# Eagle attention and MLP on one Trainium2 core: a new written order, two small loads moved to ScalarE's queue, and fewer DMA transposes

## The chip, the cores and the metric

The kernel runs on one core of a Trainium2 chip. The core has a matrix engine (TensorE, PE in the profile), three engines for elementwise work (VectorE or DVE, ScalarE or ACT, GpSimd or POOL), a sequencer that here only starts transfers (SyncE, SP), and DMA engines that move data between the chip's memory and the on-chip buffer. Each engine works through its own list of instructions in order; semaphores hold an instruction until what it needs is there. The metric is the device time of one execution in microseconds (us). Smaller is better.

## The reference

There are two stages. The first is a linear attention with a decaying state, for 4 batches, 8 heads, 768 steps and a head size of 48:

```python
for t in range(S):
    cur = einsum('bhd,bhe->bhde', u * k[t], v[t])
    y[t] = einsum('bhd,bhde->bhe', r[t], state + cur)
    state = w[..., None] * state + einsum('bhd,bhe->bhde', k[t], v[t])
```

The second takes y as rows of 384 numbers (8 heads of 48) and gives `x + relu(norm(x) @ w_ch1) @ w_ch2`, where norm subtracts the row's mean, divides by its standard deviation and multiplies by `g_ln`. The inner width is 1536. The output is 4 x 768 x 384 in float32.

## The kernel before

**Tiles.** The 768 steps of a batch are cut into 6 chunks of 128, so there are 24 chunks in all, and each chunk is a tile of 128 rows. Within a chunk the recurrence becomes matrix products: the decay is moved into the factors `Fk` and `Fr`, so that k and r only have to be multiplied by a table. A state `Z` is handed from each chunk to the next one of the same batch.

**Steps of a chunk i**, each a short function with the name used in the written order:

- LK, LR, LV load k, r and v (192 KB each, lines 315, 318, 321) on SP's queue.
- SK and SR multiply k and r by their tables (`sck`, `scr`); CV casts v to bfloat16 (`vv`). All three can be given to VectorE or GpSimd, CV to ScalarE too.
- TR turns `scr` and `sck` on TensorE (8 transposes, line 337); TC copies the result out of PSUM, or TCr and TCk half of it each (`trs`). For the chunks in `K_BY_DMA` (18 to 23) the keys are turned by a DMA instead (TKD, line 476).
- Q multiplies the turned r and k (`q`); AT forms the 128 x 128 products per head (line 356); AM masks them (line 366), for the first chunks in two halves AMa and AMb.
- S forms the diagonal term with u and the chunk's state contribution in PSUM; CC copies out the diagonal term; VB multiplies v by it on GpSimd (line 419).
- ZU takes the state contribution out of PSUM. For most chunks ZU adds the old state on VectorE (line 413) and ZD multiplies by the decay on GpSimd. For the first chunk of a batch, and for a chunk in `ZPE`, ZU is one multiplication on VectorE; for a chunk in `ZPE` the old state has been added by one more matmul in S (line 394), and there is no ZD.
- Y applies the state and the masked products (lines 429 and 437); X adds VB's result (`x`).
- ST and AG give mean and variance (lines 447 and 451), XN subtracts the mean (`xn`), and RS raises the variance to the power -1/2 on GpSimd, once for each group.
- LT turns `xn` on TensorE (3 transposes, line 481) and XT copies the result into `xT`; or LTD does both with one DMA transpose on SP's queue (line 472).

**MLP by groups.** Chunks form groups of one or two, in the list `GROUPS`. For a group, UP multiplies by the first weights (line 496): six steps of 6 matmuls with 256 columns for a group of two, three steps of 12 matmuls with 128 columns for a group of one. RL is the relu that copies 128 x 512 out of PSUM (line 512). DN multiplies by the second weights (line 524), in three parts of 4 matmuls for each chunk. OT scales by RS's result and adds x (line 534); STO stores the chunk on SP's queue. UP's number is 16 times the group plus the part, DN's is 4 times the chunk plus the part.

**Start.** WF loads w as a row, LN takes its logarithm, WBM spreads it over the partitions, FK and FR make the tables. ROWS loads w and u with head pairs down the partitions (`w_p`, `u_p`), four small transfers on SP's queue (line 214); UW and WL make from them the matrix for u and the decay table `WLZ`. LW1 loads a third of the first weights (768 KB), and SW multiplies a third of that third by -g and casts it. IW2 loads a third of the second weights from GpSimd's queue (line 312). WU and DU are matmuls of zeros that keep TensorE busy (line 260).

**The order.** There is no loop over chunks. The string `PLAN` lists every step with its number and its engine (v, s or g for VectorE, ScalarE, GpSimd; a dash where the engine is fixed), and the program emits the steps as they stand there. An engine's instructions follow in that order; each waits only for its data and its buffer. Buffers are rings whose sizes are in `SLOTS`; the change leaves them as they are.

Of the kernel before, what the change touches and what calls it, by code (L numbers as in the profile page):

```python
# [25 lines left out]
LT,0,- AT,2,- VB,1,g XT,0,s SW,2,v SW,0,s DU,3,- UP,2,- Q,2,v X,1,v UP,0,- RL,2,s
ST,1,v UP,1,- AG,1,v RL,0,s ZU,1,v RS,1,g XN,1,v DN,0,- RL,1,s AM,2,v LT,1,- DN,1,-
ZD,1,g XT,1,v S,2,- UP,16,- CC,2,v LK,3,- ZU,2,v UP,17,- VB,2,g RL,16,s LR,3,- DN,2,-
ZD,2,g SK,3,v UP,18,- OT,0,v LR,5,- Y,2,- SR,3,v DN,4,- RL,17,s LV,3,- RL,18,s X,2,v
TR,3,- DN,5,- ST,2,v LR,4,- TC,3,v DN,6,- CV,3,g AG,2,v Q,3,v LK,4,- AT,3,- XN,2,v  # L30
S,3,- SR,4,g SR,5,v LT,2,- LK,5,- XT,2,s CC,3,v RS,2,g ZU,3,v UP,32,- SK,4,v LV,5,-
UP,34,- OT,1,v RL,32,s AM,3,v TR,4,- VB,3,g LV,4,- DN,8,- CV,5,s TC,4,s SK,5,v LR,7,-
Y,3,- UP,33,- ZD,3,g X,3,v CV,4,s TR,5,- LR,6,- Q,4,v ST,3,v AT,4,- SR,7,g RL,33,s
S,4,- AM,4,v RL,34,s LK,6,- DN,9,- TC,5,s SR,6,g DN,10,- AG,3,v LK,7,- XN,3,v Y,4,-
Q,5,v LT,3,- CC,4,v AT,5,- SK,6,v RS,3,g LR,9,- XT,3,s ZU,4,v TR,6,- VB,4,g AM,5,v
S,5,- LR,16,- UP,48,- CC,5,s TC,6,s ZD,4,g UP,50,- SK,7,v LV,6,- RL,48,s X,4,v TR,7,-
VB,5,g RL,50,s OT,2,v Y,5,- LR,8,- TC,7,s UP,49,- ST,4,v X,5,v DN,12,- LK,8,- RL,49,s
AG,4,v ST,5,v AT,6,- XN,4,s Q,6,v DN,13,- LK,15,- AG,5,v AM,6,v XN,5,s RS,4,g LT,4,-
DN,14,- XT,4,s LR,10,- SK,8,g CV,6,v LT,5,- AT,7,- Q,7,v XT,5,s S,6,- SR,8,v LK,9,-
Y,6,- UP,67,- CC,6,v AM,7,v VB,6,g UP,64,- LV,7,- RL,67,s ZU,6,v TR,8,- RL,64,s X,6,v  # L40
UP,66,- LV,9,- TC,8,s SR,9,v UP,65,- CV,7,v STO,0,- RL,66,s Q,8,v AT,8,- CV,9,g LV,8,-
ST,6,v Y,7,- RL,65,s UP,68,- SK,9,v OT,3,v LK,10,- S,7,- RL,68,s TR,9,- AG,6,v SR,10,v
CC,7,s UP,69,- CV,8,s VB,7,g LR,11,- AM,8,v XN,6,s DN,16,- RL,69,s DN,17,- STO,1,- TC,9,s
ZU,7,v STO,2,- X,7,v DN,18,- ZD,7,g SK,10,v LR,13,- LT,6,- S,8,- ST,7,v XT,6,s AT,9,-
Y,8,- CC,8,v OT,4,v LR,14,- TR,10,- SR,11,g ZU,8,v DN,20,- TC,10,s AG,7,v LV,10,- Q,9,v
VB,8,g DN,21,- XN,7,v AM,9,v LT,7,- LV,17,- RS,5,g S,9,- DN,22,- XT,7,v ZD,8,g AT,10,-
LK,11,- Q,10,v UP,81,- X,8,v OT,5,v UP,80,- CC,9,s LV,11,- RL,81,s VB,9,g AM,10,v Y,9,-
RL,80,s UP,84,- LR,12,- SK,11,g ZU,9,v UP,82,- RL,84,s SR,13,v CV,11,g LK,12,- TR,11,- X,9,v
RL,82,s ZD,9,g DN,24,- ST,8,v TC,11,s LV,19,- UP,83,- CV,10,v SR,12,g AG,8,v XN,8,v Y,10,-
LV,16,- Q,11,v RL,83,s LT,8,- SK,12,g S,10,- ST,9,v UP,85,- CC,10,v AG,9,v LK,13,- ZU,10,v  # L50
XN,9,s VB,10,g DN,25,- XT,8,v RL,85,s AT,11,- LK,17,- X,10,v LT,9,- RS,6,g DN,26,- XT,9,v
AM,11,v UP,100,- LR,21,- ZD,10,g S,11,- UP,99,- SK,13,v LK,14,- RL,100,s TR,12,- CC,11,v ST,10,v
UP,101,- TC,12,v STO,3,- RL,99,s Y,11,- AG,10,v SK,14,g STO,5,- Q,12,v TR,13,- SR,14,v LR,22,-
UP,96,- TC,13,s OT,6,v SR,16,g AT,12,- XN,10,v STO,4,- DN,28,- RL,96,s AM,12,v VB,11,g LV,12,-
RL,101,s LT,10,- DN,29,- XT,10,s X,11,v UP,97,- LV,13,- ST,11,v TR,14,- RL,97,s CV,12,v UP,98,-
LV,21,- AG,11,v TC,14,v XN,11,s AT,13,- Q,13,v S,12,- LR,15,- RL,98,s AM,13,v LT,11,- Y,12,-
XT,11,s DN,30,- CC,12,s LV,15,- RS,7,g ZU,12,v UP,116,- SK,15,v UP,114,- VB,12,g LV,14,- OT,7,v
AT,14,- SR,15,v RL,114,s CV,13,g DN,32,- LK,16,- AM,14,v RL,116,s TR,15,- UP,117,- TC,15,s LV,22,-
Q,14,v UP,112,- CV,14,v X,12,v RL,117,s LR,17,- S,13,- CV,15,v Y,13,- RL,112,s ST,12,v DN,33,-
Q,15,v CV,17,g CC,13,s STO,6,- ZU,13,v UP,113,- LV,18,- VB,13,g SK,16,v S,14,- RL,113,s CV,16,v  # L60
DN,34,- AG,12,v CC,14,v LK,18,- X,13,v XN,12,s ZD,13,g TR,16,- SK,17,v AT,15,- TC,16,s LK,19,-
ST,13,v UP,115,- VB,14,g OT,8,v Y,14,- RL,115,s ZU,14,v LT,12,- LK,22,- DN,36,- XT,12,v AG,13,v
Q,16,v S,15,- RS,8,g LK,20,- DN,37,- XN,13,v SK,18,v LT,13,- DN,38,- CC,15,v XT,13,v STO,7,-
VB,15,g AM,15,v UP,128,- STO,8,- ZD,14,g LV,20,- UP,129,- RL,128,s OT,9,v AT,16,- X,14,v RL,129,s
DN,40,- LR,19,- SR,17,v Y,15,- ST,14,v DN,41,- LR,20,- AM,16,v DN,42,- STO,9,- UP,130,- X,15,v
LR,18,- OT,10,v UP,132,- SR,19,v TR,17,- LK,23,- RL,132,s AG,14,v ZU,15,v DN,44,- SR,18,g XN,14,v
RL,130,s S,16,- LK,21,- ST,15,v DN,45,- ZD,15,g CV,19,v AG,15,v UP,133,- TC,17,v LR,23,- RS,9,g
CC,16,v DN,46,- SK,19,v RL,133,s Q,17,v LTD,14,- VB,16,g UP,131,- XN,15,s CV,18,v LV,23,- OT,11,v
Y,16,- TR,18,- ZU,16,v RL,131,s DN,48,- X,16,v STO,10,- DN,49,- TCr,18,v LTD,15,- ZD,16,g SR,21,v
S,17,- TKD,18,- TR,19,- ST,16,v DN,50,- STO,11,- CV,20,v UP,149,- SR,22,v TKD,19,- TCr,19,v UP,145,-  # L70
RL,149,s OT,12,v AT,17,- AG,16,v RL,145,s CC,17,v SR,20,v DN,52,- XN,16,s AM,17,v UP,147,- VB,17,g
STO,12,- DN,53,- Q,18,v RL,147,s Y,17,- SK,20,v UP,146,- Q,19,v CV,21,v AT,18,- X,17,v DN,54,-
RL,146,s ST,17,v UP,144,- LTD,16,- OT,13,v S,18,- RL,144,s UP,148,- AG,17,v CC,18,v RS,10,g XN,17,v
# [12 lines left out]
X,22,v DN,77,- ST,22,v RL,194,s DN,78,- AG,22,v XN,22,v RS,13,g UP,197,- OT,19,v STO,18,- UP,195,-
RL,197,s DN,80,- LTD,22,- RL,195,s Y,23,- STO,19,- DN,81,- X,23,v DN,82,- ST,23,v UP,208,- AG,23,v
OT,20,v RS,14,g UP,209,- XN,23,v DN,84,- DN,85,- RL,209,s LTD,23,- RL,208,s DN,86,- UP,210,- STO,20,-
OT,21,v UP,224,- RL,210,s DN,88,- DN,89,- STO,21,- RL,224,s DN,90,- UP,225,- OT,22,v UP,226,- RL,225,s
DN,92,- RL,226,s DN,93,- STO,22,- DN,94,- OT,23,v STO,23,-  # L90
"""


@with_exitstack
def kernel(
    ctx: ExitStack,
    tc: tile.TileContext,
    r: bass.AP,
# [20 lines left out]
    FK = F // P  # L119
# [59 lines left out]
    w_p = const.tile([P, HP], FP32, name="w_p")  # L179
    u_p = const.tile([P, HP], FP32, name="u_p")  # L180
# [401 lines left out]
```

## Time and profile before

| what | value |
|---|---|
| median of 3 runs | 164.08 us (163.05 to 164.20) |
| the profiled execution, its own time | 164.15 us |
| its span in the profile | 162.4 us |
| TensorE busy | 148.9 us (92%), 1823 matmuls |
| VectorE busy | 131.5 us (81%), 282 instructions |
| ScalarE busy | 72.4 us (45%), 129 instructions |
| GpSimd busy | 73.1 us (45%), 102 instructions |
| moved by DMA | 24.48 MB, mean 151 GB/s |

The span is the time from the first to the last recorded instruction; the execution's own time is 1.75 us more. A busy TensorE is not TensorE at its peak, because each matmul is recorded with its whole passage through the array, and these overlap. In lines of groups, the numbers after the bar are the busy time of the group, the mean of one instruction in ns, and the idle time of the engine before them with what ended it. In lines of the timeline, the first two numbers are start and duration in us, and a bracket tells how long the engine stood idle before and what released it. "x12" is the number of instructions merged in one line.

### The profile page before, as it was taken

What the parts mean: (1) busy time and instruction counts of PE and PEld (TensorE: products, weight loads), DVE (VectorE), ACT (ScalarE), POOL (GpSimd) and SP (SyncE); (2) the same over time, 40 slices, a digit from 0 to 9 for tenths busy, and PEclk for the clock granted to TensorE, in tenths of its full rate; (3) what the DMA queues carried; (4) which work ended last, traced back from release to release, by engine and by line L of the source; (5) the groups of instructions that cost most, each with busy time, mean ns of one, the idle gap of its engine ahead of it and who ended that gap; (6) DMA issues with size and microseconds to landing.
All of it is one profiled execution on the core that took longest, in us unless ns stands there. A gap on an engine that the chain in (4) does not pass through costs nothing.

```text
span 162.4 us, 4487 instructions
## 1 busy us (share of the span) xinstructions
PE 148.9 (92%) x1823; PEld 120.2 (74%) x1823; DVE 131.5 (81%) x282; ACT 72.4 (45%) x129; POOL 73.1 (45%) x102
## 2 busy tenths in 40 slices
PE   7998699989999999999999899899899799999690
PEld 6797578767869868868888678678588587877570
DVE  2378777899999999999998999999998995715111
ACT  4203753438586853646566123353146152442220
POOL 3001725775844299886328637521254727211000
PEclk9999969999999999999999999999999999999998
DMA  4999997989999994994889998552322423120311
GB/s 90 220 223 257 320 215 149 213 158 179 177 199 229 240 189 97 220 261 82 178 167 219 221 202 165 125 160 57 86 71 70 77 47 117 52 73 22 105 48 48
DMA packets 88646, 24.48 MB, mean 151 GB/s; under 512 B 84017, under 2 KB 87090, under 8 KB 88626
## 3 DMA queue, kind: packets, MB, share of 16 engines
q1 hardware_dynamic: 88194, 23.02, 62.7%
q0 software_dynamic: 432, 1.18, 3.7%
q8 instruction: 14, 0.23, 0.6%
q14 instruction: 6, 0.05, 0.1%
HBM read 18.88 MB, written 4.72 MB: 145 GB/s over the span
## 4 chain that ended last, share of the span: by engine, by line
PE 40%; DVE 34%; DMA 11%; SPq 6%; issue 4%; ACT 2%; POOL 1%; DVEq 0%; POOLq 0%
PE hp L496 18%; PE o L524 15%; DMA xT<-xn 6%; DVE A L366 6%; DMA w_f<-in_moe_w_ch_dram 4%; DVE q L202 4%; DVE ot L534 4%; DVE sck L202 3%; DVE x L444 3%; DVE stats L447 3%; DVE ZS L413 3%; DVE xn L459 2%; DVE scr L202 2%; PE at L356 2%; SPq L315 1%
## 5 line engine op out<-in xcount | busy, mean ns | idle before, releaser
L512 ACT ACTIVATE hT<-hp 128x512 bf16<-128x512 f32 x72 | 42.1, 597 | 57.0 <-PE hp L496 56.1
L496 PE MATMUL hp<-xT,w_sb 128*128 128x256 bf16 (+1 forms) x540 | 57.0, 255 | 3.2 <-DMA xT<-xn 2.7
L524 PE MATMUL o<-w_sb,hT 128*128 128x384 bf16 x288 | 56.0, 326 | 1.4 <-DVE ot L534 1.4
L496 PEld LDWEIGHTS <-w_sb 128*128 128x128 bf16 x540 | 48.3, 115 | 6.8 <-DMA xT<-xn 3.2
L524 PEld LDWEIGHTS <-hT 128*128 128x128 bf16 x288 | 25.9, 97 | 14.3 <-issue 1.7
L419 POOL TENSOR_TENSOR Vb<-vf,cc 128x384 f32<-128x384 f32 x24 | 22.7, 947 | 19.2 <-DVE cc L199 14.0
L366 DVE TENSOR_TENSOR A<-at,mask 128x1024 bf16<-128x1024 f32 (+1 forms) x26 | 29.4, 1129 | 1.3 <-PE at L356 1.3
L534 DVE SCALAR_TENSOR_TENSOR ot<-o,rs,x 128x384 f32<-128x384 f32 x24 | 14.6, 609 | 12.5 <-PE o L524 12.3
L202 POOL TENSOR_TENSOR Z<-ZS,WLZ 128x384 bf16<-128x384 f32 x16 | 17.0, 1064 | 6.5 <-DVE ZS L413 6.5
L202 DVE TENSOR_TENSOR sck<-kf,Fk 128x384 bf16<-128x384 f32 x19 | 13.1, 693 | 4.0 <-ACT Fk L274 4.0
L444 DVE TENSOR_TENSOR x<-y,Vb 128x384 f32<-128x384 f32 x24 | 13.1, 547 | 3.5 <-PE y L437 2.1
L260 PE MATMUL o<-warm 128*128 128x128 bf16 x143 | 13.2, 267 | 1.0 <-DVE warm L225 1.0
L465 POOL TENSOR_SCALAR rs<-mv 128x2 f32<-128x2 f32 (+1 forms) x15 | 3.9, 259 | 22.3 <-DVE mv L451 22.1
L197 ACT COPY trs<-tr 128x1024 bf16<-128x1024 bf16 (+1 forms) x12 | 11.8, 980 | 4.5 <-PE tr L337 4.4
L260 PEld LDWEIGHTS <-warm 128*128 128x128 bf16 x143 | 11.6, 123 | 2.5 <-issue 1.3
L447 DVE BATCH_NORM_STATS2 stats<-x 128x6 f32<-128x384 f32 x24 | 13.3, 553 | 0.2
L202 DVE TENSOR_TENSOR q<-trs 128x512 bf16<-128x512 bf16 x24 | 12.5, 523 | 0.0
L468 POOL TENSOR_TENSOR rs<-rs,expo 128x2 f32<-128x2 f32 (+1 forms) x15 | 10.5, 697 | 1.2
L202 POOL TENSOR_TENSOR scr<-rf,Fr 128x384 bf16<-128x384 f32 x7 | 8.1, 1169 | 5.7 <-DMA rf<-in_r_dram 4.8
L202 DVE TENSOR_TENSOR scr<-rf,Fr 128x384 bf16<-128x384 f32 x17 | 9.7, 573 | 0.8 <-DMA rf<-in_r_dram 0.8
L356 PE MATMUL at<-trs 48*128 48x128 bf16 x192 | 9.7, 222 | 0.4 <-DMA trs<-sck 0.4
L337 PE MATMUL tr<-ident,scr 128*128 128x128 bf16 x96 | 9.5, 223 | 0.3 <-ACT xT L197 0.2
(60 smaller groups left out, 162.0 us busy)
## 6 DMA issues: line engine op xcount, KB each, us to landing
rf<-in_r_dram SPq DMA_DIRECT2D x24, 192.0 KB, 3.8
kf<-in_k_dram SPq DMA_DIRECT2D x24, 192.0 KB, 3.9
vf<-in_v_dram SPq DMA_DIRECT2D x24, 192.0 KB, 3.8
out_dram<-ot SPq DMA_DIRECT2D x24, 192.0 KB, 2.4
w_f<-in_moe_w_ch_dram SPq DMA_DIRECT2D x3, 768.0 KB, 7.2
w_sb<-in_moe_w_ch_dram POOLq DMA_DIRECT2D x3, 384.0 KB, 7.7
xT<-xn SPq DMA_TRANSPOSE x10, 2.4
trs<-sck SPq DMA_TRANSPOSE x6, 2.4
```

The costliest lines, as they stand in the source:

```text
L197: nc.scalar.copy(out=out, in_=in_)
L202: engines[e].tensor_tensor(out=out, in0=in0, in1=in1, op=ALU.mult)
L260: nc.tensor.matmul(out=warm_ps[0][:, :P], lhsT=warm[:], rhs=warm[:], start=True, stop=True)
L356: nc.tensor.matmul(out=t[:, par, q, :], lhsT=trs(i)[p0 : p0 + D, 1, q, :], rhs=trs(i)[p0 : p0 + D, 0, q, :], start=True, stop=True,)
L366: nc.vector.tensor_tensor(out=AA(i)[:, a:b].rearrange("p e q t -> p (e q) t"), in0=psum["at", i][:, a:b].rearrange("p e q t -> p (e q) t") ...
L419: nc.gpsimd.tensor_tensor(out=Vb(i)[:].rearrange("p (h d) -> p h d", h=H), in0=vf(i)[:], in1=cc(i)[:].unsqueeze(2).to_broadcast([P, H, D]) ...
L444: nc.vector.tensor_tensor(out=xx(i)[:], in0=psum["y", i][:, :C], in1=Vb(i)[:], op=ALU.add)
L447: nc.vector.bn_stats(out=stats[i % 4][:], in_=xx(i)[:])
L496: nc.tensor.matmul(out=t[:, a * gw : (a + 1) * gw], lhsT=w1_sb[n][kc][:, fb::FB], rhs=xT(g)[:, kc, :gw], start=(kc == 0), stop=(kc == CK - 1),
L512: nc.scalar.activation(out=o, in_=s, func=ACT.Relu)
L524: nc.tensor.matmul(out=psum["o", i][:, :C], lhsT=hT(g)[:, fk, j * P : (j + 1) * P], rhs=w2_sb[d][:, a, :], start=(fk == 0), stop=(fk == FK ...
L534: nc.vector.scalar_tensor_tensor(out=ot(i)[:], in0=psum["o", i][:, :C], scalar=rs[g][:, j : j + 1], in1=xx(i)[:], op0=ALU.mult, op1=ALU.add,)
```

## The change

Nothing changes in what is computed. These things do:

- `GROUPS` has 12 groups of one and 6 of two, where it had 6 and 9. The groups of one are the chunks 0 to 7 and 20 to 23.
- `ZPE` is [1, 2, 3], where it was empty.
- ROWS becomes ROWSI: the same four small transfers, u first, issued by ScalarE. It stands after LN and before FK in the order.
- LTD is not used any more: the 10 chunks 14 to 23 that it served use LT and XT like the others. TKD stays for the chunks 18 to 23.
- There are 105 matmuls of zeros instead of 143.
- The whole order is another one, and many steps have another engine:

| step | before | after |
|---|---|---|
| SK | 19 VectorE, 5 GpSimd | 12, 12 |
| SR | 17 VectorE, 7 GpSimd | 8, 16 |
| CV | 15 VectorE, 4 ScalarE, 5 GpSimd | 5, 13, 6 |
| Q | 24 VectorE | 18, 6 GpSimd |
| XN | 14 VectorE, 10 ScalarE | 3, 15, 6 GpSimd |
| XT | 6 VectorE, 8 ScalarE | 14, 10 |
| TC (whole) | 5 VectorE, 11 ScalarE | 10, 6 |
| TCr and TCk (halves) | 9 VectorE, 1 ScalarE | 3, 7 |
| CC | 15 VectorE, 9 ScalarE | 8, 16 |
| RL | 72 ScalarE | 68, 4 VectorE |
| SW | 3 VectorE, 6 ScalarE | 2, 6, 1 GpSimd |
| ZD | 16 GpSimd | 13 |
| RS | 15 GpSimd | 18 |

```diff
-GROUPS = [1, 1, 1, 1, 2, 2, 2, 2, 2, 2, 2, 2, 2, 1, 1]
-ZPE = []
+GROUPS = [1, 1, 1, 1, 1, 1, 1, 1, 2, 2, 2, 2, 2, 2, 1, 1, 1, 1]
+ZPE = [1, 2, 3]
 K_BY_DMA = [18, 19, 20, 21, 22, 23]
...
-MW,0,v WF,0,- MI,0,g TL,0,s WU,19,- LR,1,- MP,0,v MM,0,g LK,1,- LN,0,s DU,4,- WBM,0,-
-LK,0,- LR,2,- FK,0,s LR,0,- SK,0,v FR,0,s LV,0,- SK,1,v SR,0,v LK,2,- SR,1,v DU,35,-
-TR,0,- CV,0,v TCk,0,v LG,0,- TCr,0,v LV,2,- SK,2,v DU,13,- TR,1,- SR,2,v AT,0,- LW1,2,-
-TCk,1,v AMa,0,v TCr,1,v Q,0,v DU,18,- TR,2,- AMb,0,v ROWS,0,- CV,2,v LW1,1,- DU,4,- Y,0,-
-Q,1,v AT,1,- UGC,0,s UW,0,g SW,7,s SW,8,v WL,0,s AMa,1,v IW2,0,g DU,7,- S,0,- CC,0,s
-LV,1,- SW,6,s ZU,0,v VB,0,g SW,5,s LW1,0,- IW2,1,g X,0,v SW,4,s ST,0,v CV,1,s AMb,1,v
-IW2,2,g SW,3,s DU,38,- S,1,- AG,0,v TC,2,v Y,1,- XN,0,s RS,0,g SW,1,v CC,1,s DU,2,-
-LT,0,- AT,2,- VB,1,g XT,0,s SW,2,v SW,0,s DU,3,- UP,2,- Q,2,v X,1,v UP,0,- RL,2,s
...
+MW,0,v WF,0,- TL,0,s MI,0,g MP,0,v WU,13,- MM,0,g LN,0,s LK,0,- ROWSI,0,s WBM,0,- LV,1,-
+LR,0,- FK,0,s CV,1,v FR,0,s SK,0,v LK,1,- SR,0,g LR,1,- SK,1,v DU,18,- TR,0,- UW,0,g
+WL,0,s LK,2,- SR,1,g TCk,0,s LR,2,- TCr,0,s SK,2,g Q,0,v DU,22,- TR,1,- LV,0,- AT,0,-
+TCk,1,s SR,2,v LG,0,- LW1,2,- TCr,1,s AMa,0,v CV,0,g UGC,0,s AMb,0,v DU,13,- TR,2,- S,0,-
+Q,1,v TC,2,s Y,0,- AT,1,- CC,0,v ZU,0,v LV,2,- AMa,1,v VB,0,g DU,3,- S,1,- SW,7,s
+AMb,1,v LW1,1,- SW,8,s IW2,0,g X,0,v SW,6,s DU,13,- AT,2,- Q,2,v Y,1,- CV,2,g ST,0,v
+AG,0,v LW1,0,- CC,1,s XN,0,s RS,0,g ZU,1,v SW,5,s SW,3,v DU,16,- LT,0,- VB,1,g XT,0,v
+SW,4,s DU,6,- UP,2,- X,1,v S,2,- RL,2,s SW,2,g ST,1,v UP,1,- SW,0,s SW,1,v IW2,2,g
+AG,1,v AM,2,v UP,0,- XN,1,s IW2,1,g LK,3,- LT,1,- RL,1,s CC,2,v XT,1,v LR,3,- DU,1,-
+Y,2,- RL,0,s VB,2,g ZU,2,v UP,18,- SK,3,v LV,3,- DN,0,- SR,3,v RL,18,s UP,17,- X,2,v
+TR,3,- CV,3,g ST,2,v RL,17,s UP,16,- RS,1,g TC,3,v AG,2,v RL,16,s Q,3,v AT,3,- XN,2,v
+RS,2,g AM,3,v S,3,- LT,2,- DN,1,- XT,2,s CC,3,s UP,33,- ZU,3,v LK,4,- DN,2,- LV,6,-
...
-    def ROWS(i, e):
-        for src, dst in ((w, w_p), (u, u_p)):
+    def ROWSI(i, e):
+        for src, dst in ((u, u_p), (w, w_p)):
             for par in range(2):
-                nc.sync.dma_start(
+                nc.scalar.dma_start(
```

The end of the new order, from the last chunk's state on:

```diff
+STO,18,- RS,16,g UP,240,- OT,19,v LT,22,- S,23,- RL,240,s DN,80,- XT,22,s DN,81,- CC,23,s VB,23,g
+UP,257,- DN,82,- RL,257,s X,23,v STO,19,- UP,256,- OT,20,v UP,242,- ST,23,v DN,84,- AG,23,v RL,242,s
+XN,23,g DN,85,- RL,256,s RS,17,g LT,23,- DN,86,- XT,23,v UP,272,- OT,21,v UP,258,- STO,20,- DN,88,-
+RL,258,s DN,89,- RL,272,s STO,21,- DN,90,- UP,273,- OT,22,v UP,274,- RL,273,s DN,92,- RL,274,s DN,93,-
+STO,22,- DN,94,- OT,23,v STO,23,-
```

## The prediction

> **What bounds the kernel now.** I read the totals first, then the stretches, then TensorE's groups, then single waits.
>
> ```profile
> DVE  2378777899999999999998999999998995715111
> PEclk9999969999999999999999999999999999999998
> DMA  4999997989999994994889998552322423120311
> ```
>
> Slices of 4.06 us. VectorE is full from about 24 to 130 us, DMA from 4 to about 100 us, and TensorE's clock dips once, in slice 6.
>
> ```profile
> 22.30:70.00 47.70, 46.00 (x639) 37.68 (x637) 46.02 (x93) 27.01 (x47) 30.19 (x37) 0.98 0.93 189
> 70.00:112.00 42.00, 40.54 (x483) 32.51 (x478) 41.14 (x91) 19.43 (x35) 21.95 (x26) 1.00 0.76 170
> 112.00:148.00 36.00, 34.29 (x388) 27.30 (x387) 28.69 (x59) 13.41 (x24) 14.38 (x20) 1.00 0.25 68
> ```
>
> Columns: stretch, length, busy time of PE, weight loads, DVE, ACT, POOL, then clock, DMA share, GB/s. To 112 us TensorE and VectorE are both full; after that only TensorE is. Busy TensorE overstates its work, so I count work as matmuls times their spacing, which the chain of waits shows where they run back to back:
>
> ```profile
> 147.29 1.34 PE hp L496 x24
> 80.89 1.31 PE hp L496 x12
> 153.43 1.95 PE o L524 x12
> ```
>
> UP takes 56 ns with 128 columns, 109 with 256; DN 163. From the chain also: a transpose 56, AT 41; the small S and Y matmuls 25 or 42 from their starts. From 30 to 158.5 us there are 276 DN (45.0), 324 and 149 UP (35.3 and 8.3), 168 AT (6.9), 180 transposes (10.0), and 404 small ones in S and Y (12.6): 118.1 us of work in 128.5. So **TensorE loses 10.4 us** there; by the same count 6.1 of it between 30 and 112 us. Behind 112 us, waits for LTD stand out (0.75, 0.60 and 1.31 us, 2.7 in all), such as
>
> ```profile
> 152.57 0.86 PE L496 MATMUL hp<-xT,w_sb 128*128 128x128 bf16 x12 [1.31 <-DMA xT<-xn]
> ```
>
> **The start** ends at 22.4 us, when UP begins. The last third of the first weights arrives about 21.2 us (SW1 on VectorE waits for it); ScalarE's order puts XN0 behind SW5, SW4 and SW3, so TensorE has nothing to do before.
>
> **What the Trainium skill says.** "SBUF — State Buffer", Who interferes with whom: a VectorE instruction with two on-chip inputs, or in a two-port mode, and a GpSimd one shut each other out for a whole instruction; PSUM inputs don't. The trace agrees:
>
> ```profile
> 67.59 1.12 POOL L202 TENSOR_TENSOR sck<-kf,Fk 128x384 bf16<-128x384 f32 x1
> 67.76 1.22 DVE L202 TENSOR_TENSOR q<-trs 128x512 bf16<-128x512 bf16 x1
> ```
>
> Q, 0.40 us elsewhere, ends only after GpSimd's SK. "GPSIMD Engine Reference", Engine selection: two-input work is about twice as slow on GpSimd; here SR is 1.17 against 0.57 us. "DMA: Bandwidth & Descriptors", Issuing engines are not separate DMA queues: another issuing engine saves only sequencer time. The full DMA row above fits. "TensorE: Matmul & The Clock Gate", What's actually happening: the clock halves after a window of 3.4 us with too little work. Here TensorE was busy 1.50 of 3.41 us from 18.0, and the next 3.4 us ran at clock 0.52.
>
> **The change, part by part.**
>
> *Loads of w and u.* SP loses four issues of 0.42 us (1.7), which stood before the second third of the first weights. That third landed 7.2 us after its issue with DMA full, so I count no earlier weights: nine chunk loads (about 1.0 us each at some 200 GB/s), 2.36 MB of weights and the first of IW2 still fill the engines to about 21 us. ScalarE issues them after LN (end 2.72), to 4.4 us by SP's row; FK behind them waits for WBM, which with 13 zero matmuls ahead ends about 4.5 (1.64 us after LN). Hidden, zero; if an issue there took 0.8 us, FK, the first tables and all chunk-0 work slip 1.5 us, but the weights of 21 us cover that too. The gain is indirect: UW and S0 no longer wait for ROWS at 15 us, so XN0 can run about 17 us, and only UP0 has to wait for the last weights. UP2 goes at about 19, UP1 at 19.6, UP0 after SW2, which is now on GpSimd: 21.2 plus 0.8 to 1.5 us (CAST's 0.605 for 384 columns scaled to 512, or SK's 1.133), so 22.2. UP0 ends about 23 against 25.6: **2.6 us ahead**.
>
> *But IW2.* GpSimd issues the third third (IW2,2) and then the second (IW2,1) behind SW2, which waits for the last first weights; before, both were issued from 17.67 us.
>
> ```profile
> L312 POOL DMA_DIRECT2D w_sb<-in_moe_w_ch_dram x3 | 1.9, 629 | 0.3 <-issue 0.3
> DMA to landing us min/median/max: 7.3/7.7/9.1
> ```
>
> Now they are issued at about 22.0 and 22.6 us; with 7.3 us the second lands at 29.9, with an empty queue perhaps at 28. TensorE comes to DN1 after UP0, LT1, Y2, UP18, DN0, UP17, TR3, UP16, AT3, S3, LT2: 4.5 us on, at 27.5. Everything on TensorE is behind DN1. By 30.4 the old order had done DN1 and DN2 (1.3 us) where the new one has TR3, AT3, S3, LT2 (1.2): starting DN1 at 29.9 means being **0.5 us ahead**. Bounds: 2.4 ahead (landed at 27.5) to 1.5 behind (landed at 31, and the idle window halves the clock). I take 0.5.
>
> *TensorE's work* grows: ten LT more, 30 x 56 ns = 1.7; ZPE three matmuls of 384 columns, 0.5; UP 432 x 56 + 216 x 109 against 216 x 56 + 324 x 109, 0.3. The zeros lie in the start. Sum **+2.4 us**, all on the path.
>
> *VectorE.* Removed, by page means: SK 7 x 0.69, SR 9 x 0.57, CV 10 x 0.45, Q 6 x 0.52, XN 11 x 0.48, half copies 6 x 0.42, CC 7 x 0.15, SW 0.7: 27.3. Added: TC 5 x 0.67, XT 8 x 0.35, RL 4 x 0.65 (between ScalarE's 0.60 and AMa's 0.68): 8.7. Durations overlap (149 summed, 131.5 busy), so 18.6 x 0.88 = 16 us less: about 115. ZU only trades its add for a multiplication.
>
> *GpSimd.* SK 7 x 1.13, SR 9 x 1.17, Q 6 x 1.45 (0.8 by CAST, 1.5 by SK), XN 6 x 0.7 (0.6 to 1.1), RS 3 x 0.96, SW 0.9, CV 0.6, ZD less 3 x 1.06: +32, so **about 105**, two thirds of the span. VB and ZD queue behind these; X and the next Y wait for them.
>
> *ScalarE.* CC, CV, XN, XT and half copies add 13.4, five whole TC and four RL remove 7.5: +6, to 78. It idled 56 us behind UP; no cost.
>
> *LTD.* Its three waits (2.7 us) go. In its place XN, LT, XT: for the last chunk, VB 0.83, X, ST, AG, XN near 0.8, so some 3.5 us between Y23 and LT23, with UP and DN parts of 5.9 us between them: covered. SP loses ten issues of 1.2 us; what remains there late is stores.
>
> *Stalls.* Of the 10.4 us I take back 2.7 from LTD and 2.3 of the 6.1 before 112 us, where VectorE becomes loose (bounds: none, or 4). Left 5.4. LR and LK for chunks 4 to 6 still arrive only just in time, so not more.
>
> **Sum** against the profiled execution, 164.15 us (span 162.4, 1.75 around it; the median 164.08 is the same): -0.5 + 2.4 - 5.0 = -3.1, so **161.1 us**. From UP's last to the end nothing changes (3.9 us of OT and store).
>
> **Rivals.**
>
> 1. *The second weights are in time.* For: DMA has no third IW2 beside it. Against: the row of landings. The lead is 2.4 and 4 of the 6.1 come back: 164.15 - 2.4 + 2.4 - 6.7 = 157.5; half of both beyond the forecast, 159.2. I use 159.2.
> 2. *Only the work is paid for.* A tight in-order list finds new waits between small steps: half of the 5.0 comes back, 163.6, within 1%.
> 3. *GpSimd paces the middle: slower.* From VB5 to VB17 it has 9 SR, 7 SK, 12 VB, 8 ZD, 8 RS, 2 XN, 1 Q, 2 CV: 49.7 us for 12 chunks, 4.1 each, against TensorE's 5.5 (132 us of work for 24). It decides once shutting out by VectorE stretches its mean by a third. For: VB already reached 1.56 us (0.82 alone). Against: VectorE's excluding instructions fall from 89 to 46. At 5.6 per chunk over 16 chunks, 1.6 us more, with nothing recovered: 164.15 - 0.5 + 2.4 + 1.6 = 167.7.
>
> That the transposes go and the engines change is certain from the list, so no rival there.
>
> **Chances.** Forecast 0.45 (own range 159.8 to 163), the first rival 0.17, the second 0.20, the third 0.18. What a measurement here can tell from no change is about 1%: 162.4 to 165.7. Three quarters of the forecast and the first rival lie below: 0.52; the rest of it and most of the second within: 0.29; the third and a tail: 0.19. The range, 158 to 166.5, leaves out most of the third rival and the ends of the first.
>
> **What would show it.** Right: UP starts before 20 us; DN1 idles behind a DMA for w_sb near 28 to 30 us; VectorE near 115, GpSimd near 105; no DMA wait for xT; matmuls of UP 648. Wrong: if DN1 doesn't wait, the lead was bigger; if DN1 waits past 31, the start loses. If POOL lines stand ahead of Y or X in the chain through the middle, the third rival; if VectorE keeps ending TensorE's waits, the second.

## The result, and the profile after

The changed kernel takes **156.54 us** (median of 4 executions, 156.29 to 159.82), the kernel before, beside it on the same chip, 163.56 us (4 executions, 162.62 to 164.20). The ratio is 0.957, with an interval from 0.950 to 0.964: 7.0 us faster. The forecast was 161.1 us, with a range from 158.0 to 166.5, so the time lies below the range. The profiled execution took 156.55 us, with a span of 154.4 us, 8.0 us shorter than before. Three later repeats of the same kernel on other chips, told below, gained 4.2 to 4.8 us, so 2.2 to 2.8 us of the 7.0 did not come again. Medians here are over all executions, while a ratio leaves out those that lie over 1.5% above a kernel's fastest; so where a kernel's times spread widely, as for start_new, new_rows_sp and new_again_c below, the two differ. In the profile of the changed kernel every line number is one higher than before (UP is L497, DN L525, IW2 L313); in the kernels of the experiments UP is L478 or L479, DN L506 or L507.

The totals and the chain's shares by engine:

```profile
PE 146.4 (95%) x1926; PEld 118.6 (77%) x1926; DVE 119.4 (77%) x242; ACT 76.2 (49%) x149; POOL 95.7 (62%) x135
...
PE 73%; DVE 16%; DMA 3%; ACT 2%; issue 2%; SPq 1%; POOL 1%; POOLq 0%; DVEq 0%; ACTq 0%
```

The chain's shares before:

```profile
PE 40%; DVE 34%; DMA 11%; SPq 6%; issue 4%; ACT 2%; POOL 1%; DVEq 0%; POOLq 0%
```

TensorE is 73% of the chain that ended last (57 to 68% in the repeats, 40% before) and VectorE 16% (34% before). GpSimd works 95.7 us, 23 more than before, and is 1% of the chain (1 to 6% in the repeats).

The slices, here of 3.86 us:

```profile
DVE  2256989789998999999999999797797769734211
...
PEclk9999999999999999999999999999999999999998
DMA  4999999999999999989899897132153051102111
```

The dip of TensorE's clock in slice 6 is gone. DMA is still full up to slice 24, so transfers fill the first 93 us (about 100 before). VectorE has room from slice 25 on (93 us), where it was full to about 130.

The stretches, with the columns of the prediction's second fence:

```profile
17.99:21.40 3.41, 3.02 (x50) 2.51 (x47) 2.80 (x8) 2.92 (x5) 3.16 (x6) 1.00 1.15 237
30.00:70.00 40.00, 39.44 (x598) 31.58 (x596) 37.79 (x73) 20.79 (x45) 30.09 (x38) 1.00 0.99 206
70.00:112.00 42.00, 41.78 (x517) 34.15 (x515) 38.43 (x75) 23.45 (x43) 31.16 (x39) 1.00 0.68 146
112.00:150.00 38.00, 38.00 (x467) 30.52 (x465) 23.07 (x46) 15.07 (x32) 19.30 (x27) 1.00 0.24 59
```

TensorE stands for 0.8 us in all between 30 and 150 us. From 18.0 to 21.4 us, where it was busy 1.50 us before, it is now busy 3.02 us.

The start, from the timelines of GpSimd and then of TensorE (start, duration, line):

```profile
19.80 0.69 POOL L310 TENSOR_SCALAR w_sb<-w_f,g_neg 128x512 bf16<-128x512 f32 x1
20.44 1.16 POOL L313 DMA_DIRECT2D w_sb<-in_moe_w_ch_dram  x2
```

```profile
19.43 0.83 PE L497 MATMUL hp<-xT,w_sb 128*128 128x128 bf16 x12
...
20.53 0.83 PE L497 MATMUL hp<-xT,w_sb 128*128 128x128 bf16 x12
21.56 0.86 PE L497 MATMUL hp<-xT,w_sb 128*128 128x128 bf16 x12 [0.20 <-ACT w_sb L306]
...
27.59 0.81 PE L525 MATMUL o<-w_sb,hT 128*128 128x384 bf16 x4
```

UP2, UP1 and UP0 come at 19.4, 20.5 and 21.6 us, SW2 on GpSimd ends at 20.5, and the two later parts of the second weights are issued right behind it. The last line is DN1: no bracket, so no wait. The issues of IW2:

```profile
L313 POOL DMA_DIRECT2D w_sb<-in_moe_w_ch_dram x3: 537/625/786, 15.6 to 21.1; - x3
...
DMA to landing us min/median/max: 5.1/6.5/7.0
```

The last of the three, issued at 21.1 us, landed 6.5 us on, not the 7.3 us assumed. That is at 27.6 us, and DN1 began at 27.59: it went on by a hair.

The last matmuls of UP, where 1.31 us went to an LTD before:

```profile
147.42 1.50 PE L497 MATMUL hp<-xT,w_sb 128*128 128x128 bf16 x24
```

No wait. And the lock between VectorE and GpSimd, which the prediction showed with GpSimd first:

```profile
60.01 0.41 DVE L203 TENSOR_TENSOR q<-trs 128x512 bf16<-128x512 bf16 x1
60.03 1.24 POOL L203 TENSOR_TENSOR sck<-kf,Fk 128x384 bf16<-128x384 f32 x1
```

Here Q begins 0.02 us before SK, takes its plain 0.41 us, and SK is stretched to 1.24 (1.00 to 1.01 alone). The Trainium skill says the same ("SBUF — State Buffer", Who interferes with whom): which instruction is issued first decides who blocks.

**The two profiles by one count.** Matmuls times their spacing, as in the prediction, up to a time t (us):

| work done by | 30 | 40 | 70 | 112 | 150 | end |
|---|---|---|---|---|---|---|
| before | 10.0 | 18.7 | 46.2 | 85.4 | 120.9 | 127.9 |
| after | 13.2 | 22.7 | 51.4 | 92.1 | 129.7 | 130.3 |

The work is 2.4 us more (130.3 - 127.9). The start is 3.2 us ahead at 30 us (13.2 - 10.0). From 30 to 112 us TensorE loses 82.0 - 78.9 = 3.1 us where it lost 82.0 - 75.4 = 6.6; behind 112 us it loses 0.4 in the 38.6 us to the last matmul at 150.6, where it lost 4.0 in the 46.5 us to 158.5 (the prediction, which put the same count together from single steps, had 6.1 and 4.3). Stalls so give 3.5 + 3.6 = 7.1. The sum, +2.4 - 3.2 - 7.1 = -7.9, is the difference of the spans but for 0.1 us.

### The profile page after: what moved, and what is told of

Same layout as the page of the kernel before. It is cut to its first block, busy times and chain, and to the rows that moved or that the text cites. A ratio compares the mean times of both kernels' runs of the same rounds, so it can differ in the third digit from the quotient of the medians.

```text
span 154.4 us, 4697 instructions
## 1 busy us (share of the span) xinstructions
PE 146.4 (95%) x1926; PEld 118.6 (77%) x1926; DVE 119.4 (77%) x242; ACT 76.2 (49%) x149; POOL 95.7 (62%) x135
## 4 chain that ended last, share of the span: by engine, by line
PE 73%; DVE 16%; DMA 3%; ACT 2%; issue 2%; SPq 1%; POOL 1%; POOLq 0%; DVEq 0%; ACTq 0%
PE o L525 27%; PE hp L497 26%; PE tr L338 5%; PE at L357 4%; DVE A L367 4%; DMA rf<-in_r_dram 3%; PE tr L482 3%; DVE scr L203 2%; PE y L438 2%; PE s L401 2%; PE y L430 2%; PE o L261 2%; DVE x L445 2%; PE s L388 1%; DVE stats L448 1%
## 5 line engine op out<-in xcount | busy, mean ns | idle before, releaser
L497 PE MATMUL hp<-xT,w_sb 128*128 128x128 bf16 (+1 forms) x648 | 57.2, 237 | 0.3 <-ACT w_sb L306 0.2
L525 PE MATMUL o<-w_sb,hT 128*128 128x384 bf16 x288 | 57.1, 326 | 0.2 <-DVE hT L515 0.2
L497 PEld LDWEIGHTS <-w_sb 128*128 128x128 bf16 x648 | 49.4, 113 | 4.4 <-ACT w_sb L306 0.4
L525 PEld LDWEIGHTS <-hT 128*128 128x128 bf16 x288 | 25.3, 98 | 11.6 <-DVE hT L515 0.4
L420 POOL TENSOR_TENSOR Vb<-vf,cc 128x384 f32<-128x384 f32 x24 | 21.6, 898 | 12.6 <-ACT cc L198 6.7
L203 POOL TENSOR_TENSOR scr<-rf,Fr 128x384 bf16<-128x384 f32 x16 | 16.2, 1019 | 11.7 <-DMA rf<-in_r_dram 8.2
L445 DVE TENSOR_TENSOR x<-y,Vb 128x384 f32<-128x384 f32 x24 | 13.1, 547 | 4.2 <-POOL Vb L420 3.1
L203 POOL TENSOR_TENSOR Z<-ZS,WLZ 128x384 bf16<-128x384 f32 x13 | 13.6, 1048 | 2.5 <-DVE ZS L414 2.3
L198 ACT COPY trs<-tr 128x512 bf16<-128x512 bf16 (+1 forms) x13 | 10.0, 782 | 10.5 <-PE tr L338 10.5
L203 POOL TENSOR_TENSOR sck<-kf,Fk 128x384 bf16<-128x384 f32 x12 | 12.6, 1046 | 0.3 <-PE s L401 0.3
L469 POOL TENSOR_TENSOR rs<-rs,expo 128x1 f32<-128x1 f32 (+1 forms) x18 | 10.9, 603 | 1.5
L203 DVE TENSOR_TENSOR sck<-kf,Fk 128x384 bf16<-128x384 f32 x12 | 9.6, 799 | 1.4 <-DMA kf<-in_k_dram 1.4
L203 DVE TENSOR_TENSOR q<-trs 128x512 bf16<-128x512 bf16 x18 | 8.8, 489 | 2.4 <-ACT trs L198 2.4
L261 PEld LDWEIGHTS <-warm 128*128 128x128 bf16 x105 | 8.7, 124 | 2.4 <-issue 1.3
L458 ACT ACTIVATE xn<-x,mv 128x384 bf16<-128x384 f32 x15 | 9.2, 613 | 2.5 <-DVE mv L452 2.5
```

What stands on the lines that cost most here:

```text
L203: engines[e].tensor_tensor(out=out, in0=in0, in1=in1, op=ALU.mult)
L261: nc.tensor.matmul(out=warm_ps[0][:, :P], lhsT=warm[:], rhs=warm[:], start=True, stop=True)
L420: nc.gpsimd.tensor_tensor(out=Vb(i)[:].rearrange("p (h d) -> p h d", h=H), in0=vf(i)[:], in1=cc(i)[:].unsqueeze(2).to_broadcast([P, H, D]) ...
L445: nc.vector.tensor_tensor(out=xx(i)[:], in0=psum["y", i][:, :C], in1=Vb(i)[:], op=ALU.add)
L497: nc.tensor.matmul(out=t[:, a * gw : (a + 1) * gw], lhsT=w1_sb[n][kc][:, fb::FB], rhs=xT(g)[:, kc, :gw], start=(kc == 0), stop=(kc == CK - 1),
L525: nc.tensor.matmul(out=psum["o", i][:, :C], lhsT=hT(g)[:, fk, j * P : (j + 1) * P], rhs=w2_sb[d][:, a, :], start=(fk == 0), stop=(fk == FK ...
```

## The experiments

Each ratio is against runs of the kernel before that were taken beside it on the same chip; its interval stands in brackets. The first theory is the prediction's: a little from the start, more from an unloaded VectorE and the missing LTD. Rivals are named in the expectations. In the cuts of the plans, dots stand for what is left out.

### The two halves of the change

start_new: the new order up to TR of chunk 3, the old order from there.

```diff
-GROUPS = [1, 1, 1, 1, 1, 1, 1, 1, 2, 2, 2, 2, 2, 2, 1, 1, 1, 1]
-ZPE = [1, 2, 3]
+GROUPS = [1, 1, 1, 1, 2, 2, 2, 2, 2, 2, 2, 2, 2, 1, 1]
+ZPE = [1, 2]
...
-UP,17,- X,2,v TR,3,- CV,3,g ST,2,v RL,17,s UP,16,- RS,1,g TC,3,v AG,2,v
+UP,17,- X,2,v RS,1,g DN,1,- UP,16,- RL,16,s DN,2,- OT,0,v LR,5,- DN,4,-
```

> The new order, with its two ZPE chunks 1 and 2 and ScalarE's loads of w and u, up to the transposes of chunk 3 (TR3); behind that the old order, groups and engines, LTD with them. Theory (the start itself is worth 3.2 us by counting matmul work done at 30 us): 160.5 to 161.5 us. Rival (the start is worth only the 0.5 us of the prediction, the rest comes from the middle and end): 163 to 164.

166.81 us, ratio 1.004 [0.997, 1.012]: no gain. The same kernel on another chip:

> The run with the new start and the old rest once more, for a profile in which the weights come on time. Theory (the start leads by 2 to 3 us of matmul work at 30 us, and the VectorE-bound middle of the old order takes it back): the lead is below 1 us at 112 us; some 161 to 163 us. Rival (the new start doesn't lead in front of the old rest at all): no lead at 30 us either.

165.33 us, ratio 1.018 [1.010, 1.026], two executions. Here the last third of the first weights landed at 19.9 us, as early as in the changed kernel, and at 22 us TensorE had done 6.1 us of work (3.6 before). At 30 us it had 10.0, no more than the shown execution of before and 1.1 less than the other kernels with the old start. What lies between, from TensorE's timeline and then from the stretches:

```profile
27.77 1.34 PE L506 MATMUL o<-w_sb,hT 128*128 128x384 bf16 x4 [2.75 <-DMA w_sb<-in_moe_w_ch_dram]
```

```profile
27.00:31.00 4.00, 3.23 (x19) 2.29 (x19) 0.00 (x0) 0.57 (x2) 1.00 (x1) 0.61 1.05 203
```

This is the wait of the prediction's paragraph on IW2. Behind the join the old order has DN1 right behind UP17, while UP16, TR3, AT3, S3 and LT2 stand ahead of it in the new one. So TensorE comes to DN1 at 25.0 us, stands 2.75 us, and the clock halves on top (0.61 in the mean of these 4 us). The late issue of IW2 costs what the prediction feared, unless the order has other work ahead of DN1. The new order has it, and comes to DN1 at 27.6 us instead of 25.0.

rest_new: the old start, the new order from TR3 on.

```diff
-ZPE = [1, 2, 3]
+ZPE = [3]
...
-MW,0,v WF,0,- TL,0,s MI,0,g MP,0,v WU,13,- MM,0,g LN,0,s LK,0,- ROWSI,0,s WBM,0,- LV,1,-
+MW,0,v WF,0,- MI,0,g TL,0,s WU,19,- LR,1,- MP,0,v MM,0,g LK,1,- LN,0,s DU,4,- WBM,0,-
...
```

> The reverse: the old order up to TR3 with ROWS on SyncE's queue and no ZPE but chunk 3, behind that the new order, groups and engines, no LTD. Theory (7.2 us fewer stalls behind 30 us less 2.2 us more work): 158.5 to 159.5 us. Rival (the prediction's 5.0 less 2.4): 161 to 162.

159.96 us, ratio 0.985 [0.977, 0.993]. The rest alone is worth 2.4 to 2.9 us on its chip (162.83 before). The expectations were times against the 164.15 us of the profile; as differences they are some 5 us (theory) and 2.6 us (rival), so this is the rival's size. The trace has 7.9 us of work from 30 to 40 us, where the changed kernel has 9.5: the old start costs behind the join too. The start alone is worth nothing, so its part of the gain needs the new order behind it. How large that part is was not measured on one chip.

### The middle: which engine has the small steps

new_engines_old: the new order, but the 51 steps of SK, SR, CV, Q and XN from chunk 3 on that had changed their engine have the old one (43 of them go back to VectorE).

```diff
-SR,5,g
+SR,5,v
...
-SK,6,g
+SK,6,v
...
-Q,13,g
+Q,13,v
...
```

> The new kernel in its new order, with the old engines for SK, SR, Q, XN and CV of the chunks 3 to 23. Theory (the relief of VectorE is what makes the middle dense): VectorE near 130 us, 159 to 162 us. Rival (the order alone does it, VectorE had room): 156 to 157.5.

165.29 us, ratio 1.014 [1.004, 1.024]. That is 2.5 us slower than before, and slower than either expectation. The traced execution took 166.18 us and had the last of its first weights late, at 22.0 us, so it is read only from 40 us on. The stretch from 40 to 112 us, of this kernel and then of the changed one:

```profile
40.00:112.00 72.00, 67.10 (x918) 53.80 (x917) 71.05 (x143) 33.21 (x63) 42.00 (x53) 1.00 0.78 169
```

```profile
40.00:112.00 72.00, 71.50 (x978) 58.38 (x973) 67.10 (x130) 41.06 (x80) 56.08 (x70) 1.00 0.80 172
```

With 71.05 us of VectorE in 72, TensorE (the first number after the length) falls from 71.5 to 67.1 us.

new_sk_sr_old takes back the engines of SK and SR alone, new_q_xn_old those of Q and XN.

```diff
-SR,5,g
+SR,5,v
...
-SK,6,g
+SK,6,v
...
```

> The changed kernel with the old engines for SK and SR alone (15 go back to VectorE, 2 to GpSimd, some 7 us of VectorE work). Theory (VectorE's load in the middle decides): 2 to 4 us over the changed kernel. Rival (it is where the steps stand on the way to TensorE that decides, and SK and SR can be done early): within 1 us.

160.81 us, ratio 0.982 [0.977, 0.988], VectorE at 125.0 us.

```diff
-XN,3,g
+XN,3,v
...
-Q,13,g
+Q,13,v
...
```

> The changed kernel with the old engines for Q and XN alone (some 8 us more on VectorE, as much as the run with SK and SR). Theory (load): 2 to 4 us over the changed kernel, as with SK and SR. Rival (place in the chain): 3 to 6 us over it, as Q and XN stand directly ahead of TensorE's S, AT's successor and LT.

161.62 us, ratio 0.994 [0.990, 0.997], VectorE at 127.9 us. On the same chip as both the changed kernel took 157.99 us, ratio 0.972 (below). By the ratios the pairs so cost 1.7 and 3.6 us (2.8 and 3.6 by the medians); the interval of the first just meets that of the changed kernel, [0.966, 0.978]. The trace of new_q_xn_old is of an execution of 164.46 us that had lost 3 us by 40 us. In work done from 40 to 112 us:

| kernel | work, us | against the repeat |
|---|---|---|
| changed kernel, repeat b | 68.9 | |
| changed kernel, its other three traces | 67.5 to 69.5 | -1.4 to 0.6 |
| SK and SR as before | 66.6 | -2.3 |
| Q and XN as before | 65.4 | -3.5 |
| all five as before | 63.3 | -5.6 |

The two parts nearly add up to the whole (5.8 against 5.6). VectorE is busy 119.8 us in repeat b and 125.0, 127.9 and 132.6 us in the three, so each us of its load costs 0.43 to 0.44 us of TensorE's work. These are single traces, and the first loss is little more than the changed kernel's own spread; the other two are well beyond it. In this order the load of VectorE so sets TensorE's pace from 40 to 112 us, and GpSimd's added work costs nothing that shows: the rival in which GpSimd paces the middle is refuted.

old_engines_new: the same 51 steps, with the new engines in the old order.

```diff
-SR,5,v
+SR,5,g
...
-SK,6,v
+SK,6,g
...
-Q,13,v
+Q,13,g
...
```

> The old kernel in its old order, with the new engines for SK, SR, Q, XN and CV of the chunks 3 to 23. Theory (less VectorE work is worth something in itself): 1 to 3 us under the old kernel. Rival (the engine only pays with an order made for it; GpSimd's slower steps stand too late in the old order): 1 to 6 us over it.

164.56 us, ratio 1.010 [1.008, 1.012]: 1% slower, with VectorE at 119.0 us instead of 131.5. From 40 to 112 us TensorE did 65.5 us of work, 66.7 before. So an unloaded VectorE is worth nothing in the old order. POOL's share of the chain is 10% there and 1 to 6% in the four traces of the changed kernel: in the old order the slower GpSimd steps are waited for. That the new order starts them early enough is argued from this, not measured by itself.

### LTD and the groups

new_ltd: the changed kernel with the DMA transposes of chunks 14 to 23 put back.

```diff
-LT,14,- ... XT,14,v
+LTD,14,-
```

> The new kernel with LTD in the place of LT and without XT for the chunks 14 to 23, seven groups. TensorE has 1.7 us less work. Theory (each transfer takes 2.4 to 3.8 us and the order leaves about 1 us between LT and UP): some 1 to 2 us of waiting per group, 163 to 170 us. Rival (LTD costs only where it cost before, three waits of 2.7 us in all, less 1.7 us of work): 157 to 158.

163.70 us, ratio 1.000 [0.996, 1.004]: the whole gain is gone. From 112 to 150 us TensorE did 31.5 us of work instead of 37.6. The waits it has for xT:

```profile
PE hp L478 <- DMA xT<-xn: 5.4, 5, 2.3
```

Five waits, 5.4 us (the columns are total, times, longest). The transposes stand here where LT stood; an order that starts them earlier was not tried.

old_lt: the old kernel without LTD.

```diff
-LTD,14,-
+LT,14,- XT,14,s
```

> The old kernel with LT in the place of LTD for the chunks 14 to 23 and XT on ScalarE directly behind it; all else as it was. Theory (2.7 us of waits go, 1.7 us of transposes come): 0.5 to 1.5 us under the old kernel. Rival (the waits are taken over by others, VectorE and the shared PSUM tile among them): within 0.5 us of it or above.

163.99 us, ratio 1.005 [1.002, 1.007]. LTD's waits of 2.7 us go, LT adds 1.7 us of work to TensorE, and the time doesn't fall: the old order loses at least the rest elsewhere.

old_singles: the old order with the new groups only. A pair's six parts of UP become two times three.

```diff
-GROUPS = [1, 1, 1, 1, 2, 2, 2, 2, 2, 2, 2, 2, 2, 1, 1]
+GROUPS = [1, 1, 1, 1, 1, 1, 1, 1, 2, 2, 2, 2, 2, 2, 1, 1, 1, 1]
```

> The old kernel with the new groups (one each for the chunks 4 to 7, 20 and 21) and its old order otherwise; UP and RL of a pair are shared out in their old places. Theory (256 columns at 109 ns cost what twice 128 at 56 cost, and the groups are only a freedom for the order): within 0.7 us of the old kernel. Rival (smaller groups pay in themselves, as UP needs one chunk less): 1 us or more under it.

159.97 us, ratio 0.983 [0.977, 0.988]: 2.6 us faster, which I had not expected. Its wait for xT is

```profile
PE hp L478 <- DMA xT<-xn: 0.6, 1, 0.6
```

against 2.7 us in three waits before. Those of 0.75 us (at 117.25) and of 1.31 us (at 152.57) are gone, but that isn't the groups' direct doing: all three waits belong to the UP of chunks 17, 19 and 23, whose groups are the same in both kernels. The issue of LTD23, before and here:

```profile
148.73 2.68 SPq L472 DMA_TRANSPOSE xT<-xn  x1
```

```profile
145.96 1.19 SPq L454 DMA_TRANSPOSE xT<-xn  x1
```

It landed 3.8 us after the start of its issue before and 2.3 us here, and so did LTD17; LTD19 took 2.35 us in both, and its wait is there in both (0.60 and 0.62 us). So 2.1 of the 2.7 us that the prediction put down to LTD hung on two slow landings in one execution; why these were slow is open. Where the gain of 2.6 us comes from is open too. By the count of work, 1.1 us of the lead stands already at 30 us, ahead of every group that differs (why is told with the prediction's start below), 0.7 comes from 40 to 112 us, which is within the spread of single traces, and 1.2 from 112 to 150 us, where the two landings are.

### The start: loads, SW2 and chance

new_again, with new_again_b and new_again_c: the changed kernel, once more on three other chips.

> The changed kernel unaltered, on the chip of the next three. The first third of the second weights is issued while the last third of the first weights is still on its way. Theory (that last third ends near 19.5 us in some executions and 2 to 3 us later in others, and SW2, the other two thirds of the second weights and DN1 follow it): times in two clusters, 156.3 to 157 us and 159 to 161 us; the profile of the second kind has DN1 wait 2 to 4 us for w_sb as the prediction had it. Rival (no such split): all within 0.5% of 156.5 us.

158.94 us against 163.19, ratio 0.974 [0.970, 0.978]. Neither came: the six times lie close together, from 158.25 to 159.71 us, all above 156.5.

> The changed kernel unaltered, as the measure for the next three on their chip: 156.3 to 159.5 us.

157.99 us against 162.58, ratio 0.972 [0.966, 0.978].

> The changed kernel once more, beside its form without ZPE on the same chip. It was 156.5, 158.9 and 158.0 us so far. Both views expect 156 to 159.5 here, with the first weights' last third in by 20 us and DN1 at 27.5 to 28.3 us.

158.91 us (156.66 to 160.15) against 163.72, ratio 0.963 [0.956, 0.970]. DN1 in the profiles of the first and of the second repeat:

```profile
28.23 0.81 PE L507 MATMUL o<-w_sb,hT 128*128 128x384 bf16 x4 [0.61 <-DMA w_sb<-in_moe_w_ch_dram]
```

```profile
27.88 0.81 PE L507 MATMUL o<-w_sb,hT 128*128 128x384 bf16 x4 [0.72 <-DMA w_sb<-in_moe_w_ch_dram]
```

The third waits 0.72 us too, at 27.62. So the wait that was predicted is there, at 0.6 to 0.7 us, and absent by a hair in the profile shown above. The rest of the spread was not followed through; one place is a late v for a cast on GpSimd in the first repeat:

```profile
90.71 0.50 POOL L182 CAST vv<-vf 128x384 bf16<-128x384 f32 x1 [3.56 <-DMA vf<-in_v_dram]
```

From 70 to 112 us that execution did 39.0 us of work, the shown one 40.7. That the late v is the reason is argued from this.

new_sw2_v: SW2 on VectorE, behind SW1, so that GpSimd can issue IW2 without waiting for the first weights.

```diff
-SW,2,g ST,1,v UP,1,- SW,0,s SW,1,v IW2,2,g
+ST,1,v UP,1,- SW,0,s SW,1,v SW,2,v IW2,2,g
```

> The changed kernel with SW2 on VectorE directly behind SW1 instead of on GpSimd, so that the last two thirds of the second weights (IW2) are issued without waiting for the last third of the first weights. Theory (the prediction's mechanism: IW2 behind SW2 makes DN1 wait where those weights come late): no wait of DN1 for w_sb, 0.3 to 2 us under the changed kernel, its slow executions most. Rival (the second weights then take DMA from the last third of the first, which ends later and holds UP0): 0 to 2 us over it.

158.90 us, ratio 0.977 [0.972, 0.982], where the changed kernel beside it took 157.99: no gain. IW2 was issued by 18.9 us instead of 21.2 and DN1's wait is gone. In its place:

```profile
27.52 0.61 PE L320 MATMUL tr<-ident,scr 128*128 128x128 bf16 x4 [2.83 <-DVE scr L185]
```

TR3 stands 2.83 us for chunk 3's `scr`, which VectorE makes when r has come:

```profile
26.90 0.56 DVE L185 TENSOR_TENSOR scr<-rf,Fr 128x384 bf16<-128x384 f32 x1 [3.39 <-DMA rf<-in_r_dram]
```

In the changed kernel the same step runs at 23.83. The second weights were issued earlier, and this r, issued ahead of them at 12.9 us, took 14.0 us to land; in new_again_b it was issued at 13.1 us and took 10.1. The start is a row of transfers that share full DMA engines (share 1.06 from 10 to 20 us in new_again_c); changing the order of one changed which step waits.

new_rows_sp: the four small loads from SP's queue, at the place where ScalarE has them.

```diff
-                nc.scalar.dma_start(
+                nc.sync.dma_start(
```

> The changed kernel with the four small loads of w and u issued by SyncE at the same place in the order. Theory (the engines of DMA are full, an issue 1.7 us later on SyncE's queue only moves the first chunk loads and is covered): within 0.6 us of the changed kernel. Rival (SyncE's issue time is on the path at the start): 1 to 2 us over it.

161.55 us (158.62 to 164.68), ratio 0.977 [0.973, 0.980]; and once more:

> The run with the four small loads issued by SyncE once more, for a profile in which the weights come on time. Theory (DMA idles about 1 us while SyncE issues them, and everything behind on its queue comes that much later): the thirds of the first weights end 1 to 2 us later than with ScalarE's issue, the lead at 30 us is 1 to 2 us smaller. Rival (other transfers fill in): the same ends within 0.5 us.

158.51 us, ratio 0.976 [0.971, 0.981], two executions. By the ratios nothing is lost that can be told (0.974 and 0.972 in the repeats). But 13 of the first 20 times are 161.3 us or more, while the changed kernel's six beside them end at 159.7; what lies behind that spread is open. The trace shows the step. The stretch from 4 to 5 us of new_rows_sp_b and, in the second fence, of new_again_c:

```profile
4.00:5.00 1.00, 1.00 (x9) 0.81 (x9) 0.00 (x0) 0.63 (x2) 0.00 (x0) 1.00 0.35 25
```

```profile
4.00:5.00 1.00, 1.00 (x9) 0.76 (x9) 0.00 (x0) 0.58 (x2) 0.00 (x0) 1.00 1.17 190
```

SP issues the four from 1.61 to 3.64 us; the DMA engines (share and GB/s are the last columns) fall to 0.35 from 4 to 5 us, the loads of r behind land 0.9 to 1.2 us later, and the first weights 1.5 to 1.8 us later (their last third at 21.1 against 19.6 us). TensorE has 11.7 us of work at 30 us, 12.6 to 13.2 in the repeats. At 150 us it has 127.5, as much as the first repeat (127.4) and 1.2 to 2.0 us less than the other two, so whether it makes the late start good isn't settled.

new_zpe_none: without ZPE; ZD comes back for chunks 1 to 3.

```diff
-ZPE = [1, 2, 3]
+ZPE = []
...
-ZU,1,v
+ZU,1,v ZD,1,g
```

> The changed kernel with ZPE empty: three matmuls of 0.16 us less on TensorE, and three ZD of 1.05 us more on GpSimd at the start, directly behind their ZU. Theory (the state is needed by the next Y and GpSimd issues the second weights meanwhile): 0.5 to 2 us over the changed kernel. Rival (GpSimd has room): within 0.5 us of it.

157.17 us, ratio 0.968 [0.964, 0.971]; and beside the changed kernel on one chip:

> The changed kernel without ZPE: for chunks 1 to 3 ZU adds the old state on VectorE and GpSimd multiplies by the decay (three more ZD), and TensorE is spared three matmuls of 384 columns (0.5 us). View A, ZPE earns nothing: within 0.7 us of the run beside it, or up to 1 us faster by the spared work. View B, ZPE keeps the states of the first chunks off VectorE and GpSimd where those are late: 1 us or more slower than the run beside it, and the low 157.17 us seen before was the execution's luck with its weights.

159.65 us against 158.91, ratios 0.976 [0.970, 0.982] and 0.963 [0.956, 0.970]. On this chip that favours ZPE, by 0.7 us in the medians and 1.3% in the ratios, whose intervals meet at 0.970; the 0.968 of the first run stands against 0.974 for the changed kernel on that chip, the other way round. So ZPE's worth is not settled. It is not the start's gain: without it TensorE has 12.1 to 12.4 us of work at 30 us, with it 12.6 to 13.2, of which 0.5 are ZPE's own three matmuls. No version here is clearly better than the changed kernel.

## Why the prediction was wrong in size, step by step

**What failed** is two terms of the sum, both with the right sign. The sum had -0.5 (start), +2.4 (work), -5.0 (stalls); measured in the shown profiles are -3.2, +2.4, -7.1. Part of this is the luck of two executions: the repeats gained 4.2 to 4.8 us where the forecast had 3.1, and their medians, 158.0 to 158.9 us, lie at the lower end of its range.

**The start.** The failing step is "SW2 ... 21.2 plus 0.8 to 1.5 us, so 22.2", with "issued at about 22.0 and 22.6 us" behind it: the landing of the first weights was taken from one execution as if it were fixed. It was 21.2 us in that execution. In the four experiments that keep the old start (rest_new, old_lt, old_engines_new, old_singles) it was 19.4 to 20.2 us; in the changed kernel's shown profile it was 19.7. So "I count no earlier weights" was right about the change, and the start number wrong about the weights: SW2 ended at 20.5, the issues came at 20.4 and 21.1 us, the landing took 6.5 us instead of 7.3, and DN1, which TensorE reached at 27.6 (predicted 27.5), went on. The wait itself was real: 0.6 to 0.7 us in the repeats, 2.75 where the order came to DN1 at 25.0 us.

The 3.2 us themselves fall into two parts. The four kernels with the old start had 11.0 to 11.2 us of work at 30 us and no halved clock, the shown execution of before 10.0 with it: 1.1 us of the lead belongs to that execution, with its late weights and its halved clock, which the prediction named (1.50 us busy of 3.41) but left out of its sum. The other 1.5 to 2.1 us (12.6 to 13.2 against 11.1) come with the new start, 0.5 of them as ZPE's matmuls. The prediction's sum has a slip there: it charged these 0.5 us as work on the path, though they stand ahead of DN1, whose time it took from a landing. Counted as work done, its start was -1.0 and not -0.5, still far from -3.2.

**The stalls.** "2.3 of the 6.1 before 112 us" was 3.5 of 6.6, within its bounds of none and 4; "2.7 from LTD" was 3.6 behind 112 us. The reason given for the cautious middle, loads of r and k that still arrive just in time, weighed too much for this execution: TensorE stands 0.8 us in all between 30 and 150 us. The first repeat, with its late v, did lose 1.7 us from 70 to 112 us. The engines decide there in the new order, as the experiments on the middle show.

**LTD.** Right that its waits go and that XN, LT and XT in its place are covered: no wait for xT by a DMA is left, and putting LTD back costs the whole gain. But 2.7 us was no price that belongs to LTD. In the old order its removal is worth nothing, and 2.1 of the 2.7 us were two slow landings of the one execution that was profiled.

**ROWS.** Right: ScalarE's four issues, 2.04 to 3.91 us, stand where FK waits for WBM anyway. From ScalarE's timeline:

```profile
2.04 0.88 ACTq L215 DMA_DIRECT2D u_p<-in_u_dram  x2
2.95 0.96 ACTq L215 DMA_DIRECT2D w_p<-in_w_dram  x2
4.35 0.58 ACT L275 ACTIVATE Fk<-y,pow_i 128x384 f32<-128x384 f32 x1 [1.80 <-PE y L271]
```

**The engines' sums.** VectorE 119.4 us (115 predicted): its own SK took 0.80 instead of 0.69, RL 0.68 instead of 0.65. GpSimd 95.7 (105): Q took 1.16 instead of the 1.45 taken between two rows, SR 1.02 instead of 1.17, SK 1.05 instead of 1.13. ScalarE 76.2 (78). UP has 648 matmuls, as said.

**The rivals.** The first, with the second weights in time and 4 us of the middle back, named 157.5 us as its full size; it is what the shown execution did, and it had a chance of 0.17. The repeats (0.963, 0.972 and 0.974) lie between it (157.5 of 164.15, 0.959) and the forecast (0.981). The second, new waits between small steps, is what happened to the old order with the new engines, not to the new one. The third did not occur.

**Open.** Why the first weights, and a transpose here and there, land late in some executions; what the new groups do for the old order; and whether IW2,1, which DN1 needs, would end the wait if issued ahead of IW2,2. That was not tried.

## What to carry to other kernels

An engine's relief, a removed transfer and an order of instructions are no separate sums here: the new engines of 51 steps cost 1% in the old order, old engines in the new order cost 1.4% against before, and both together gain 2.6 to 4.3%. So test a part inside the new order before saying what it is worth. And take the landing times of transfers, of a large load as of a transpose, from several executions; a forecast that hangs on one landing should carry the spread of it in its sum.

## What the runs showed of the hardware

- The last third of the first weights (768 KB) landed at 19.3 to 20.2 us in ten profiles of kernels with the new start, and at 21.5, 22.0 and 22.8 us in three, with the same transfers ahead of it. The second weights then land at 30.2 to 31.6 us. The cause was not found.
- The ten DMA transposes of `xn` in the profile of before landed 2.3 to 3.8 us after the start of their issue (median 2.4). Behind two of 3.8 us TensorE stood 0.75 and 1.31 us.
- Four issues of small loads (0.8 KB each) took SP 2.0 us at the front of its queue, left the DMA engines at a share of 0.35 for a microsecond, and the thirds of the first weights came 1.5 to 1.8 us late. The Trainium skill ("DMA: Bandwidth & Descriptors", Issuing engines are not separate DMA queues) says that another issuing engine saves only the sequencer's time, usually small; here that time was a gap in the transfers, on which the end of the kernel did not measurably depend by the ratios.
